# Operand addresses, a stage hand-over and a weight conversion with a part on GpSimd

## The chip, the cores and the metric

The kernel runs on one core of a Trainium2 chip. The metric is the device time of one execution in microseconds, as the median of several runs. The engines are called TensorE (PE), VectorE (DVE), ScalarE (ACT), GpSimd (POOL) and SyncE (SP, which issues all DMAs here).

## The reference

Three blocks follow each other; everything is float32, the weights come as float64.

```python
# attention: 8 batches, 8 heads, 576 tokens, head size 64; keys and values averaged over 8 tokens (72 remain)
attn = softmax(q @ mean8(k).T / 8)
x = attn @ mean8(v)                       # -> 4608 tokens x 512
# first block, d_ff = 768
h = maximum(maximum(x @ w1, x @ w2), x @ w3)
x = h @ w_out                             # 4608 x 512
# second block, d_ff = 2048
h = x @ w_in
out = (h - tanh(h)) @ w_out2              # 4608 x 512
```

## The kernel before

**Precision.** TensorE takes float32r operands. So every operand is kept as two tiles, H (the value rounded to float32r) and L (the rest), and each product is three matmuls, H with H, H with L and L with H, added up in one PSUM accumulator. A tile is split by a copy on ScalarE (H) and a subtraction on VectorE or GpSimd (L).

**Weight conversion** (`conv`, L74 to L90). A float64 weight tile arrives as pairs of 32-bit words (`raw`, 128x512 pairs, two buffers, loaded by `conv_load`). VectorE cuts the exponent out (L78), ScalarE turns it into a float32 exponent (L80), VectorE builds mantissa and sign (L81, L83, L85) and ORs the exponent in (L87); ScalarE rounds to H (L89), GpSimd subtracts to L (L90). `pe` and `ma` have two buffers each. One call does a whole tile; 18 tiles of w1, w2, w3, 6 of the first w_out and 32 of the second block go through it.

**Stages.**
- First stage (to about 628 us): the attention, tile by tile of up to 128 tokens, and the three products of the first block, in 12 blocks of 384 tokens. One product of 128 output columns is a "group" (`moe_group`, L466): 12 matmuls of 384 columns (L476 to L478), then a copy or a maximum (L480, L482). `moe_part` (L489) interleaves the groups with the attention's steps. Ahead of a group it calls `conv_next`, which converts one tile; `CONV_LEAD = 2` tiles are converted ahead of the first group. The first 18 groups are two blocks' first nine each, and need the nine first weight tiles alone. The six tiles of the first w_out are converted in the last block's groups.
- Middle stage (L540 to L604): 9 blocks of 512 tokens, `acc[e] += wo[kc] * h[kc]`, 72 matmuls of 512 columns a block (L592 to L594) in 6 steps kc. The h tiles come back from DRAM by `load_split` (L558), four steps ahead, and are split two steps ahead (ScalarE L566, VectorE L567). The sums go out by L598 and L600 and the DMA L601 into xs. Even blocks accumulate in the PSUM pool psm, odd ones in ps2. In the same loop `conv_c` converts the 32 tiles of the second block, evenly over the steps.
- Last stage (L612 on): 9 blocks of 512 tokens by 16 chunks of 128 hidden columns: `h2` (L657, 12 matmuls into one accumulator of pool psc), the activation `gact` (L631, 4 operations of ScalarE, 7 of VectorE and the cast L650), and `prod` three chunks later (L667, 4 sums of 3 matmuls). Its x tiles are loaded by `c_load` and split by `c_split`, the L part on GpSimd; those of the first block right at the start of the stage (L687 to L690), the others one block ahead.

**Order.** Each engine and each DMA queue runs its list in order. The lists are made by the framework, which takes an instruction as soon as its model of the program holds it ready, in the order of the source otherwise; so instructions of a later source line can stand ahead of others. Waits are put in from the tiles that are read and written.

**Addresses.** Tiles lie in stacks from both ends of a partition's memory. The first 16,384 bytes are a scratch area for DMA descriptors. Pools of the left side (consts, wH, wL, xH, xL, h, the conversion's buffers of the first stage, and the second block's weights ct) follow upwards: all operands of TensorE on this side start at 192 mod 512 bytes. Pools of the right side (the attention's `at`, then io, wo, the conversion's buffers of the middle stage, gp) go down from the end: io, wo and gp (ioH, ioL, woH, woL, gH, gL) all start at 480 mod 512. The attention's tiles are of other sizes, so their starts differ among themselves (VH, VL at 96, eH, eL, eX at 352).
In the groups both operands lie left, in the middle stage both right. In `h2` the stationary tile is ct (left) and the moving one io (right), in `prod` the stationary tile is gp's (right) and the moving one ct (left).

Of the kernel before, what the change touches and what calls it, by code (L numbers as in the profile page):

```python
# [36 lines left out]
CONV_LEAD = 2  # L37
# [10 lines left out]
def moe_chain_kernel(ctx, tc, qt, kt, vm, vl, ident, cst, w123, wo1, win, wout, out):  # L48
# [19 lines left out]
    # float64 words to float32, split into two float32r parts  # L68
    def conv_load(st, src):
        raw = st.tile([128, 512, 2], I32, tag="raw", name="raw", bufs=2)  # L70
        Q.dma_start(out=raw.bitcast(I64).rearrange("p n o -> p (n o)"), in_=src)
        return raw

    def conv(st, raw, H, L, eng):  # L74
        pe = st.tile([128, 512], I32, tag="pe", name="pe", bufs=2)
        a = st.tile([128, 512], I32, tag="ma", name="ma", bufs=2)
        lo, hi = raw[:, :, 0], raw[:, :, 1]
        V.tensor_scalar(out=pe, in0=hi, scalar1=20, scalar2=0x7FF,  # L78
                        op0=ALU.logical_shift_right, op1=ALU.bitwise_and)
        A.activation(pe, pe, AF.Relu, bias=ebias, scale=float(1 << 23))  # L80
        V.tensor_scalar(out=a, in0=hi, scalar1=3, scalar2=0x7FFFFF,  # L81
                        op0=ALU.logical_shift_left, op1=ALU.bitwise_and)
        V.scalar_tensor_tensor(out=a, in0=hi, scalar=-2147483648, in1=a,  # L83
                               op0=ALU.bitwise_and, op1=ALU.bitwise_or)
        V.scalar_tensor_tensor(out=a, in0=lo, scalar=29, in1=a,  # L85
                               op0=ALU.logical_shift_right, op1=ALU.bitwise_or)
        V.tensor_tensor(out=a, in0=a, in1=pe, op=ALU.bitwise_or)  # L87
        w = a.bitcast(F32)
        A.copy(H, w)  # L89
        eng.tensor_tensor(out=L, in0=w, in1=H.bitcast(F32), op=ALU.subtract)  # L90

# [5 lines left out]
    sta = pool("sta")  # L97
    at = pool("at", side="right")
# [18 lines left out]
    # attention units: (first token, tiles of tokens); a tile is (batch, first token in batch, count)  # L117
# [201 lines left out]
    # one list of steps for the whole attention, in the order in which they are issued  # L319
# [87 lines left out]
    # v of a batch may be replaced once its last product is issued  # L407
# [17 lines left out]
    # startup  # L425
# [10 lines left out]
    raws = {0: conv_load(sta, w123[0])}  # L436
    Q.dma_start(out=idt, in_=ident)
    raws[1] = conv_load(sta, w123[1])
# [4 lines left out]
    nconv = [0]  # L443

    def conv_next():
        i = nconv[0]
        if i < 18:
            conv(sta, raws.pop(i), wH[i].rearrange("p a b -> p (a b)"),
                 wL[i].rearrange("p a b -> p (a b)"), G)
            nconv[0] += 1  # L450
            if i + 2 < 18:
                raws[i + 2] = conv_load(sta, w123[i + 2])

# [9 lines left out]
    for _ in range(CONV_LEAD):  # L463
        conv_next()
# [24 lines left out]
    def moe_part(groups, upto):  # L489
        """groups of products, with the attention's steps up to upto spread over them"""  # L490
        first = pos[0]

        def pace(x):
            attn_to(first + (upto - first) * x // (2 * len(groups)))

        for k, (j, f, m) in enumerate(groups):
            conv_next()
            moe_group(j, f, m, lambda: pace(2 * k + 1))
            pace(2 * k + 2)
# [6 lines left out]
    def point(x):  # L506
        """the step at which the attention is x blocks far"""
# [7 lines left out]
    moe_part(gr(1, 0, HF), point(2.5))  # L515
# [9 lines left out]
    raws = {i: conv_load(sta, wo1[i]) for i in range(2)}  # L525
    nconv[0] = 0

    def conv_next():
        i = nconv[0]
        if i < NF:  # L530
            conv(sta, raws.pop(i), woH[i], woL[i], G)
            nconv[0] += 1
            if i + 2 < NF:
                raws[i + 2] = conv_load(sta, wo1[i + 2])

# [9 lines left out]
    # pairs in the order of use: input chunk c, output chunk c  # L545
    srcs = [(win if c % 2 == 0 else wout)[c // 2] for c in range(2 * NC2)]
    raws = {i: conv_load(stb, srcs[i]) for i in range(2)}
    nconv = [0]

    def conv_c():  # L550
        i = nconv[0]
        if i < 2 * NC2:
            conv(stb, raws.pop(i), wt[i][0], wt[i][1], G)
            nconv[0] += 1
            if i + 2 < 2 * NC2:
                raws[i + 2] = conv_load(stb, srcs[i + 2])
# [18 lines left out]

    loads = [(j, kc) for j in range(NB) for kc in range(NF)]
# [6 lines left out]
    for i, (j, kc) in enumerate(loads):  # L583
        if kc == 0:
            acc = [psm.tile([128, 512], F32, tag="mm", name="ps_mm") if j % 2 == 0 else
                   ps2.tile([128, 512], F32, tag="sc" if e < 2 else "tr", name="ps_acc") for e in range(NE)]
# [17 lines left out]
        while nconv[0] < min(2 * NC2, (i + 1) * 2 * NC2 // (len(loads) - 2)):  # L604
            conv_c()
# [7 lines left out]
    gp = pool("gp", bufs=2, side="right")  # L613
    xl_ = [(j, kc) for j in range(NB) for kc in range(NE)]
    lt = {}
    nld, nsp = [0], [0]

    def c_load():
# [145 lines left out]
```

## Time and profile before

| | |
|---|---|
| median of 3 runs | 1607.62 us (1607.29 to 1608.44) |
| span of the profiled execution | 1608.5 us |
| another time of that execution | none is shown |
| TensorE busy | 1548.1 us (96%) |
| VectorE busy | 1215.2 us (76%) |
| ScalarE busy | 836.4 us (52%) |
| GpSimd busy | 223.7 us (14%) |

The span is cut into 40 slices of 40.2 us; a digit is the busy share of a slice in tenths (9 is 90% or more), and PEclk the clock granted to TensorE in tenths of full speed.

```profile
PE   4789999999999999998899999999999999999999
DVE  8999565555555663999588878788888888887886
POOL 5351210202010011332301001010101001010000
PEclk9899999999999999999999999999999999999999
```

A matmul's profiled duration overlaps the next one's, so what a matmul costs is read from the distance of starts, or from the number of matmuls in a stretch without idle time. Likewise an instruction of VectorE that is held up by another engine shows as a longer one.

### The profile page before, as it was taken

What the parts mean: (1) busy time and instruction counts of PE and PEld (TensorE: products, weight loads), DVE (VectorE), ACT (ScalarE), POOL (GpSimd) and SP (SyncE); (2) the same over time, 40 slices, a digit from 0 to 9 for tenths busy, and PEclk for the clock granted to TensorE, in tenths of its full rate; (3) what the DMA queues carried; (4) which work ended last, traced back from release to release, by engine and by line L of the source; (5) the groups of instructions that cost most, each with busy time, mean ns of one, the idle gap of its engine ahead of it and who ended that gap; (6) DMA issues with size and microseconds to landing.
All of it is one profiled execution on the core that took longest, in us unless ns stands there. A gap on an engine that the chain in (4) does not pass through costs nothing.

```text
span 1608.5 us, 21497 instructions
## 1 busy us (share of the span) xinstructions
PE 1548.1 (96%) x7540; PEld 1337.7 (83%) x7540; DVE 1215.2 (76%) x2131; ACT 836.4 (52%) x2081; POOL 223.7 (14%) x245
## 2 busy tenths in 40 slices
PE   4789999999999999998899999999999999999999
PEld 4688999999999999876688888888888888888887
DVE  8999565555555663999588878788888888887886
ACT  5565455545545521444465555555555555555554
POOL 5351210202010011332301001010101001010000
PEclk9899999999999999999999999999999999999999
DMA  7455232212121232676500001010100000010000
GB/s 236 158 161 163 84 99 79 87 45 75 42 65 39 67 120 77 230 241 234 198 1 27 26 2 52 1 53 0 33 21 27 26 27 27 1 54 0 27 1 27
DMA packets 61997, 117.87 MB, mean 73 GB/s; under 512 B 10816, under 2 KB 20160, under 8 KB 61888
## 3 DMA queue, kind: packets, MB, share of 16 engines
q1 hardware_dynamic: 61888, 116.49, 21.8%
q8 instruction: 59, 0.97, 0.3%
q14 instruction: 50, 0.41, 0.1%
HBM read 83.43 MB, written 33.03 MB: 72 GB/s over the span
## 4 chain that ended last, share of the span: by engine, by line
PE 50%; DVE 0%; issue 0%
PE ps_mm L663 8%; PE ps_mm L662 8%; PE ps_mm L664 8%; PE ps_acc L676 8%; PE ps_acc L675 8%; PE ps_acc L677 8%; DVE ob L683 0%
## 5 line engine op out<-in xcount | busy, mean ns | idle before, releaser
L476 PE MATMUL ps_mm<-xH,wH 128*128 128x384 f32 x864 | 304.5, 353 | 5.3 <-ACT wH L89 4.5
L477 PE MATMUL ps_mm<-xL,wH 128*128 128x384 f32 x864 | 292.4, 339 | 1.0 <-DVE xL L317 1.0
L478 PE MATMUL ps_mm<-xH,wL 128*128 128x384 f32 x864 | 292.7, 339 | 0.6 <-POOL wL L90 0.6
L650 ACT CAST gH<-w 128x512 fp32r<-128x512 f32 x144 | 89.4, 621 | 297.0 <-DVE w L649 297.0
L662 PE MATMUL ps_mm<-ioH,ctH 128*128 128x512 f32 x576 | 228.3, 396 | 5.3 <-ACT ob L598 5.3
L663 PE MATMUL ps_mm<-ioL,ctH 128*128 128x512 f32 x576 | 229.1, 398 | 0.0
L664 PE MATMUL ps_mm<-ioH,ctL 128*128 128x512 f32 x576 | 228.5, 397 | 0.0
L675 PE MATMUL ps_acc<-ctH,gH 128*128 128x512 f32 x576 | 228.1, 396 | 0.0
L676 PE MATMUL ps_acc<-ctL,gH 128*128 128x512 f32 x576 | 227.9, 396 | 0.0
L677 PE MATMUL ps_acc<-ctH,gL 128*128 128x512 f32 x576 | 227.9, 396 | 0.0
L651 DVE TENSOR_TENSOR gL<-w,gH 128x512 fp32r<-128x512 f32 x144 | 104.1, 723 | 92.5 <-ACT gH L650 92.3
L476 PEld LDWEIGHTS ps_mm<-xH,wH 128*128 128x128 f32 x864 | 164.7, 191 | 7.2 <-ACT wH L89 4.8
L477 PEld LDWEIGHTS ps_mm<-xL,wH 128*128 128x128 f32 x864 | 164.6, 191 | 1.9 <-DVE xL L317 1.7
L478 PEld LDWEIGHTS ps_mm<-xH,wL 128*128 128x128 f32 x864 | 163.7, 189 | 1.5 <-POOL wL L90 1.5
L567 POOL TENSOR_TENSOR ioL<-ioL,ioH 128x512 fp32r<-128x512 f32 x36 | 53.5, 1509 | 666.9 <-ACT ioH L566 666.9
L662 PEld LDWEIGHTS ps_mm<-ioH,ctH 128*128 128x128 f32 x576 | 108.6, 189 | 32.2 <-ACT ob L598 5.7
L663 PEld LDWEIGHTS ps_mm<-ioL,ctH 128*128 128x128 f32 x576 | 108.7, 189 | 27.1
L664 PEld LDWEIGHTS ps_mm<-ioH,ctL 128*128 128x128 f32 x576 | 108.8, 189 | 26.0
L675 PEld LDWEIGHTS ps_acc<-ctH,gH 128*128 128x128 f32 x576 | 108.2, 188 | 26.5
L677 PEld LDWEIGHTS ps_acc<-ctH,gL 128*128 128x128 f32 x576 | 108.2, 188 | 26.5
L676 PEld LDWEIGHTS ps_acc<-ctL,gH 128*128 128x128 f32 x576 | 108.2, 188 | 25.8
L482 DVE TENSOR_TENSOR h<-h,ps_mm 128x384 f32<-128x384 f32 x144 | 79.0, 549 | 66.0 <-PE ps_mm L478 59.2
(108 smaller groups left out, 2924.9 us busy)
## 6 DMA issues: line engine op xcount, KB each, us to landing
hs<-h SPq DMA_DIRECT2D x72, 192.0 KB, 1.9
ioL<-hs SPq DMA_DIRECT2D x54, 256.0 KB, 4.2
kraw<-kt SPq DMA_DIRECT2D x32, 288.0 KB, 3.9
raw<-w SPq DMA_DIRECT2D x18, 512.0 KB, 3.5
xs<-ob SPq DMA_DIRECT2D x36, 256.0 KB, 2.6
ioL<-xs SPq DMA_DIRECT2D x36, 256.0 KB, 3.0
out<-ob SPq DMA_DIRECT2D x36, 256.0 KB, 2.2
qraw<-qt SPq DMA_DIRECT2D x32, 256.0 KB, 2.7
```

The source lines that it names most:

```text
L476: T.matmul(ps[:, :BA], wH[i][:, kc], xh[:, kc], start=(kc == 0), stop=False)
L477: T.matmul(ps[:, :BA], wH[i][:, kc], xl[:, kc], start=False, stop=False)
L478: T.matmul(ps[:, :BA], wL[i][:, kc], xh[:, kc], start=False, stop=(kc == NE - 1))
L482: V.tensor_tensor(out=t, in0=t, in1=ps[:, :BA], op=ALU.max)
L650: A.copy(gH, w)
L651: V.tensor_tensor(out=gL, in0=w, in1=gH.bitcast(F32), op=ALU.subtract)
L662: T.matmul(ps, wh[:, kc], xh, start=(kc == 0), stop=False)
L663: T.matmul(ps, wh[:, kc], xl2, start=False, stop=False)
L664: T.matmul(ps, wl_[:, kc], xh, start=False, stop=(kc == NE - 1))
L675: T.matmul(acc, gH[:, r], oh, start=(c == 0), stop=False)
L676: T.matmul(acc, gH[:, r], ol, start=False, stop=False)
L677: T.matmul(acc, gL[:, r], oh, start=False, stop=(c == NC2 - 1))
```

## The change

- **Addresses.** A tile of 72 floats (288 bytes a partition), used by nothing, is put at the bottom of the right side, so that all tiles there start 288 bytes lower: io, wo and gp at 192 mod 512, as the left side does. The scratch area for DMA descriptors becomes 1,024 bytes instead of 16,384 (both multiples of 512).
- **Conversion in three steps** (class `Conv`). `bits` is L78 to L85 with the exponent on ScalarE, `join` adds the exponent on GpSimd (an int32 add in the place of VectorE's OR, L87), `split` is the copy to H on ScalarE and the subtraction on GpSimd. A call of `step` splits tile i-2, takes the bits of tile i, loads tile i+2 and joins tile i-1. `pe` has three buffers and `ma` four.
- **Pace.** `CONV_LEAD` is 4 steps. In the second nine groups a step is made ahead of every second group.
- **First tiles of the last stage.** In the last four steps of the middle stage `c_load(V)` loads the four x tiles of block 0, and in the last two `c_split` splits them, the L part on VectorE; the calls ahead of the last stage are gone.
- **PSUM.** In the middle stage even blocks accumulate in ps2 and odd ones in psm; the last block is an even one.

```diff
-CONV_LEAD = 2
+CONV_LEAD = 4
...
+    class Conv:
+        def __init__(self, st, srcs, outs):
+            self.st, self.srcs, self.outs, self.n = st, srcs, outs, len(srcs)
+            self.raws, self.w, self.i = {}, {}, 0
+            for i in range(2):
+                self.load(i)
...
+        def bits(self, i):
+            raw = self.raws.pop(i)
+            pe = self.st.tile([128, 512], I32, tag="pe", name="pe", bufs=3)
+            a = self.st.tile([128, 512], I32, tag="ma", name="ma", bufs=4)
...
+        def join(self, i):
+            a, pe = self.w[i]
+            G.tensor_tensor(out=a, in0=a, in1=pe, op=ALU.add)
+
+        def split(self, i):
+            w = self.w.pop(i)[0].bitcast(F32)
+            H, L = self.outs[i]
+            A.copy(H, w)
+            G.tensor_tensor(out=L, in0=w, in1=H.bitcast(F32), op=ALU.subtract)
+
+        def step(self):
+            i = self.i
+            if i >= self.n + 2:
+                return
+            if i - 2 >= 0:
+                self.split(i - 2)
+            if i < self.n:
+                self.bits(i)
+                self.load(i + 2)
+            if 0 <= i - 1 < self.n:
+                self.join(i - 1)
+            self.i += 1
...
+    pool("rp", side="right").tile([128, 72], F32, name="rpad")
     at = pool("at", side="right")
...
         for k, (j, f, m) in enumerate(groups):
-            conv_next()
+            if k % every == 0:
+                cv.step()
...
-    moe_part(gr(1, 0, HF), point(2.5))
+    moe_part(gr(1, 0, HF), point(2.5), 2)
...
-            acc = [psm.tile([128, 512], F32, tag="mm", name="ps_mm") if j % 2 == 0 else
+            acc = [psm.tile([128, 512], F32, tag="mm", name="ps_mm") if j % 2 else
...
         if i + AHEAD < len(loads):
             lt[i + AHEAD] = load_split(hsrc(*loads[i + AHEAD]), V)
-        while nconv[0] < min(2 * NC2, (i + 1) * 2 * NC2 // (len(loads) - 2)):
-            conv_c()
+        else:
+            c_load(V)
+        if i >= len(loads) - 2:
+            c_split()
+            c_split()
+        while cv.i < min(cv.n + 2, (i + 1) * (cv.n + 2) // (len(loads) - 2)):
+            cv.step()
...
-    for _ in range(4):
-        c_load()
-    for _ in range(4):
-        c_split()
...
-    nc = bacc.Bacc("TRN2", target_bir_lowering=False, num_devices=1)
+    nc = bacc.Bacc("TRN2", target_bir_lowering=False, num_devices=1, dynamic_dma_scratch_size=1024)
```

## Rows read from the trace of the kernel before

**Rows 1.** The page's first lines: span, busy us, share, instructions by engine.

```profile
span 1608.5 us, 21497 instructions
...
PE 1548.1 (96%) x7540; PEld 1337.7 (83%) x7540; DVE 1215.2 (76%) x2131; ACT 836.4 (52%) x2081; POOL 223.7 (14%) x245
```

**Rows 2.** Three stretches: busy us (x instructions) by engine, TensorE's granted clock, DMA.

```profile
40.00:160.00 120.00, 100.69 (x551) 93.02 (x551) 116.73 (x234) 72.56 (x250) 44.00 (x49) 0.90 0.50 160
...
560.00:600.00 40.00, 39.14 (x224) 38.55 (x224) 26.85 (x47) 12.20 (x22) 8.05 (x4) 1.00 0.40 136
628.10:789.50 161.40, 152.31 (x648) 120.17 (x648) 148.13 (x213) 72.55 (x124) 48.94 (x33) 1.00 0.65 223
```

**Rows 3.** Waits of TensorE, 628 to 790 us: total us, times, longest.

```profile
PE ps_mm L593 <- DVE ioL L567: 4.1, 6, 1.5
PE ps_acc L593 <- DVE ioL L567: 4.0, 7, 1.5
```

**Rows 4.** The same columns in three stretches where TensorE never waits.

```profile
600.00:626.00 26.00, 26.00 (x152) 26.00 (x151) 4.43 (x8) 1.93 (x4) 0.00 (x0) 1.00 0.09 31
632.00:700.00 68.00, 68.00 (x302) 56.31 (x301) 65.19 (x93) 30.81 (x53) 22.74 (x15) 1.00 0.67 228
820.00:1590.00 770.00, 770.00 (x3301) 619.30 (x3300) 632.51 (x982) 423.39 (x735) 44.81 (x29) 1.00 0.06 21
```

**Rows 5.** Groups of TensorE instructions: busy us, mean ns of one, idle us before.

```profile
L675 PE MATMUL ps_acc<-ctH,gH 128*128 128x512 f32 x576 | 228.1, 396 | 0.0
...
L594 PE MATMUL ps_mm<-ioH,woL 128*128 128x512 f32 x120 | 46.8, 390 | 0.0
```

**Rows 6.** Timeline around the last stage's start: start us, us, engine, line.

```profile
787.02 2.73 SPq L561 DMA_DIRECT2D ioL<-xs  x6
...
789.54 0.39 PE L594 MATMUL ps_mm<-ioH,woL 128*128 128x512 f32 x1
...
790.88 3.30 ACT L566 CAST ioH<-ioL 128x512 fp32r<-128x512 f32 x5 [6.17 <-DMA ioL<-xs]
...
795.21 0.79 PE L662 MATMUL ps_mm<-ioH,ctH 128*128 128x512 f32 x1 [5.27 <-ACT ob L598]
```

**Rows 7.** Busy times and granted clock (PEclk) behind that start.

```profile
795.30:801.20 5.90, 5.90 (x14) 4.64 (x15) 0.00 (x0) 0.71 (x2) 3.70 (x3) 0.50 0.67 222
```

**Rows 8.** Groups of VectorE and GpSimd instructions, 628 to 790 us.

```profile
L90 POOL TENSOR_TENSOR ctL<-ma,ctH 128x512 fp32r<-128x512 f32 x32 | 47.6, 1490 | 157.8 <-ACT ctH L89 157.8
...
L567 DVE TENSOR_TENSOR ioL<-ioL,ioH 128x512 fp32r<-128x512 f32 x47 | 44.2, 943 | 6.8 <-ACT ioH L566 6.8
...
L85 DVE SCALAR_TENSOR_TENSOR ma<-raw,ma 128x512 int32<-128x512 int32 x30 | 26.5, 883 | 0.6
...
L81 DVE TENSOR_SCALAR ma<-raw 128x512 int32<-128x512 int32 x30 | 22.4, 746 | 1.2 <-POOL ctL L90 1.2
...
L87 DVE TENSOR_TENSOR ma<-ma,pe 128x512 int32<-128x512 int32 x30 | 20.5, 682 | 0.5
```

**Rows 9.** Single lines: duration ns min/median/max, first and last start.

```profile
L81 DVE TENSOR_SCALAR ma<-raw x56: 409/418/1520, 14.4 to 778.5; 128x512 int32<-128x512 int32 x56
...
L85 DVE SCALAR_TENSOR_TENSOR ma<-raw,ma x56: 672/691/1776, 16.4 to 779.6; 128x512 int32<-128x512 int32 x56
...
L567 DVE TENSOR_TENSOR ioL<-ioL,ioH x54: 674/684/1795, 562.0 to 784.0; 128x512 fp32r<-128x512 f32 x54
...
L90 POOL TENSOR_TENSOR ctL<-ma,ctH x32: 1282/1358/1826, 632.3 to 782.3; 128x512 fp32r<-128x512 f32 x32
```

**Rows 10.** Timelines of VectorE and GpSimd at 652 us.

```profile
652.27 1.51 DVE L81 TENSOR_SCALAR ma<-raw 128x512 int32<-128x512 int32 x1
...
652.14 1.35 POOL L90 TENSOR_TENSOR ctL<-ma,ctH 128x512 fp32r<-128x512 f32 x1 [3.68 <-ACT ctH L89]
```

**Rows 11.** Timeline of TensorE at 335 us: an av product.

```profile
335.31 0.34 PE L309 MATMUL ps_av<-eH,VH 128*128 128x384 f32 x1
...
336.01 0.34 PE L476 MATMUL ps_mm<-xH,wH 128*128 128x384 f32 x1
```

More of the change, by code (lines that the diff above doesn't have):

```diff
@@ L66, in moe_chain_kernel @@
     xs = [dr.tile([NE, 128, BB], F32, name=f"xs{i}") for i in range(NB)]
[L69 to L90, printed above, removed]
@@ L435, in moe_chain_kernel @@
     next_v()
-    raws = {0: conv_load(sta, w123[0])}
+    cv = Conv(sta, [w123[i] for i in range(18)],
+              [tuple(t[i].rearrange("p a b -> p (a b)") for t in (wH, wL)) for i in range(18)])
     Q.dma_start(out=idt, in_=ident)
-    raws[1] = conv_load(sta, w123[1])
     q_split(0)
@@ L487, in moe_chain_kernel, with moe_part @@
     hsb = {}
-    def moe_part(groups, upto):
+    def moe_part(groups, upto, every=1):
         first = pos[0]
@@ L524, in moe_chain_kernel @@
     woL = [wo.tile([128, 512], F32R, name=f"woL{i}") for i in range(NF)]
[L525 to L534, printed above, removed]
+    cv = Conv(sta, [wo1[i] for i in range(NF)], list(zip(woH, woL)))
     moe_part(gr(NA - 1), pos[0])
@@ L546, in moe_chain_kernel @@
     srcs = [(win if c % 2 == 0 else wout)[c // 2] for c in range(2 * NC2)]
[L547 to L556, printed above, removed]
+    cv = Conv(stb, srcs, wt)
     def load_split(src, eng):
@@ L574, in hsrc, with c_load, c_split @@
         return hs[g][kc][:, o:o + BB]
+    xl_ = [(j, kc) for j in range(NB) for kc in range(NE)]
+    ct = {}
+    nld, nsp = [0], [0]
+    def c_load(eng):
+        i = nld[0]
+        if i < len(xl_):
+            j, kc = xl_[i]
+            ct[i] = load_split(xs[j][kc], eng)
+            nld[0] += 1
+    def c_split():
+        i = nsp[0]
+        if i < len(xl_):
+            ct[i][1]()
+            nsp[0] += 1
     loads = [(j, kc) for j in range(NB) for kc in range(NF)]
@@ L603, in moe_chain_kernel @@
             lt[i + AHEAD] = load_split(hsrc(*loads[i + AHEAD]), V)
-        while nconv[0] < min(2 * NC2, (i + 1) * 2 * NC2 // (len(loads) - 2)):
-            conv_c()
+        else:
[4 more added lines that the diff above has]
+        while cv.i < min(cv.n + 2, (i + 1) * (cv.n + 2) // (len(loads) - 2)):
+            cv.step()
     close("stb")
@@ L613, in moe_chain_kernel @@
     gp = pool("gp", bufs=2, side="right")
[L614 to L618, printed above, removed]
-        i = nld[0]
-        if i < len(xl_):
-            j, kc = xl_[i]
-            lt[i] = load_split(xs[j][kc], G)
-            nld[0] += 1
-    def c_split():
-        i = nsp[0]
-        if i < len(xl_):
-            lt[i][1]()
-            nsp[0] += 1
     def gact(ps):
@@ L660, in h2 @@
         for kc in range(NE):
[L661 removed]
+            xh, xl2 = ct[j * NE + kc][0]
             T.matmul(ps, wh[:, kc], xh, start=(kc == 0), stop=False)
@@ L701, in moe_chain_kernel @@
                 for _ in range(NE):
-                    c_load()
+                    c_load(G)
             if 6 <= c < 10:
@@ L706, in moe_chain_kernel @@
                 for k in range(NE):
-                    lt.pop(j * NE + k)
-    for nme in ("psc", "gp", "io", "wl", "cst"):
+                    ct.pop(j * NE + k)
+    for nme in ("psc", "gp", "io", "rp", "wl", "cst"):
         close(nme)
```

27 lines of the change are left out of this document (16 added, 11 removed).

## The prediction

> **What bounds the kernel now.** I read the summary first: TensorE is busy 1548.1 of 1608.5 us [rows 1], so whatever is won must come from matmuls that run faster or from places where they wait. A change of about 0.2% (3 us) is what a measurement here can tell from none. The 40 slices, which stand with the times, show TensorE short of full at the start and around the middle stage (the second product). The busy times of those stretches say who is full there: VectorE, 116.7 of 120 us from 40 to 160 us; and in the middle stage, 628.1 to 789.5 us, 148.1 of 161.4 us, where TensorE's 648 matmuls need less [rows 2]. What TensorE waits for there is VectorE's split L567, 8.1 us in 13 waits [rows 3]. So the start and the middle stage go at VectorE's pace. The last stage (from 795 us) is TensorE alone: 3301 matmuls of 512 columns are counted in 770 us, the first already running, without a gap: one each 233.3 ns [rows 4].
>
> The middle stage has matmuls of the same form, and in its first stretch, where nothing waits, 302 are counted in 68 us, two of them already running: one each 226.7 ns [rows 4]. In clocks of 2.4 GHz that is 544 against 560 for the same 512 columns. One difference between the two stages is where operands lie: in the middle stage stationary and moving tiles are both on the right side (480 mod 512), in the last stage one of them lies left (192) and the other right (480).
>
> **The change, part by part.**
>
> *Addresses.* The pad of 288 bytes moves every right-side tile from 480 to 192 mod 512, so in the last stage the two operands agree as they do in the middle stage. The last stage has 6 groups of 576 matmuls, 3456 in all [rows 5]. Nothing in the trace of before shows that stage with equal addresses: its slot is bounded by 233.3 ns (nothing gained) and 226.7 ns (the middle stage's). I take 226.7, since the nearest row has the same columns, the same weight loads and the same triplets of products: 3456 x 6.67 ns = **-23.0 us**. VectorE is no new bound: it is busy 632.5 of 770 us there [rows 4], and a stage 3% shorter leaves it near 85%. In the first two stages the operands of a matmul all move together or not at all, so nothing changes there. The smaller descriptor area only gives room; no DMA here comes from GpSimd.
>
> What the 6.67 ns are is not seen in the trace, and the Trainium skill speaks against it: "TensorE: Matmul & The Clock Gate", step-by-step section of part 2, has two independent read ports, so that loading the next weights takes no read bandwidth from the running matmul. By that rule the sum loses its 23.0 us; the two rates of rows 4 differ all the same.
>
> *Hand-over to the last stage.* Before, TensorE stands 5.27 us in front of the first L662 matmul, put down to ScalarE's output copies L598; ahead of those in its queue are five casts L566 that waited 6.17 us for the loads from xs, issued at 787.02, 2.5 us ahead of the last L594 [rows 6]. Then the granted clock is 0.50, the lower level, from 795.3 to 801.2 us: 14 matmuls in 5.9 us instead of 3.3 at 233 ns, so 2.6 us more [rows 7]. After the change these four loads and their splits are issued in the last four steps of the middle stage, and the last block's sums lie in the other PSUM pool, so that the first accumulator of the last stage has long been free. On SP's queue the loads pass the last block's stores, which nobody awaits, and still stand behind those of the block before. Two of the four splits follow VectorE's last output copies: I leave 2 x 0.6 = 1.2 us of waiting for them and take -5.3 - 2.6 + 1.2 = **-6.7 us** (bounds: 0 if the wait stays, -7.9).
>
> *Joining on GpSimd, middle stage.* VectorE loses L87, 32 times 0.68 us: -21.8 us [rows 8]. GpSimd gets 32 more instructions of the kind of L90 (1.36 us median, 1.49 mean) [rows 8, 9]. They are not free for VectorE: while a GpSimd product runs, VectorE's next instruction is held. At 652.14 us L90 starts, and L81, which has a median of 0.42 us, takes 1.51 us [rows 9, 10]. Summed over the stage, mean against undisturbed median of the three lines most hit: L81 30 x (746 - 418), L85 30 x (883 - 691), L567 47 x (943 - 684) ns, together 27.8 us for 32 GpSimd products [rows 8, 9]: 0.87 us each. TensorE needs 648 x 226.7 ns = 146.9 of the stage's 161.4 us and VectorE paces the rest, so what VectorE gains or loses I put on the stage in full. A join's price has never been seen; bounds are 0 (it falls where VectorE reads PSUM or is idle) and 1.49 (held for a whole mean L90). I take 0.87, the mean of a like instruction in the same stage: 32 x (0.87 - 0.68) = +6.1 us. Two more tiles can be through VectorE's four steps before the stage begins (four "ma" buffers instead of two, and VectorE has a third of 560 to 600 us free [rows 2]): 2 x 2.2 = -4.4; four splits of the last stage's tiles now run here: 4 x 0.68 = +2.7. Sum **+4.4 us**. The wait that joins add is GpSimd's on ScalarE's L80; a step later ScalarE's cast waits for the join, with casts L566 behind it in its queue. One whole step of run-up, about 5 us (161.4 / 32), hides both.
>
> The Trainium skill, "SBUF — State Buffer", section on who interferes with whom, says that of a VectorE instruction with two SBUF inputs and a GpSimd one that reads SBUF the second is blocked fully. By that a join would cost up to its whole 1.36 us and this stage +20 us instead of +4.4; rows 10 show 1.09 us, since the instruction in flight goes on.
>
> *Joining on GpSimd, start.* 18 tiles at the same price: 18 x (0.87 - 0.68) = **+3.4 us** (bounds 18 x -0.68 = -12.2 and 18 x 0.81 = +14.6). Four lead steps give as many finished tiles ahead of each group as two whole conversions did, and spreading the second nine groups' steps moves no VectorE work past 160 us: nothing. The six tiles of woH fall where VectorE has room (26.9 of 40 us) [rows 2]: nothing; were that room gone, 6 x 0.19.
>
> *Sum.* -23.0 - 6.7 + 4.4 + 3.4 = -21.9 us on the profiled execution. Its span is 1608.5, 0.9 us above the median of the runs (1607.62) and 0.1 above the slowest; no other end-to-end time is shown for it. On the median: **1585.7 us**.
>
> **The rivals.**
> 1. *Addresses do nothing.* The slot of 233.3 ns comes from something else of the last stage. For: the av products of the first stage have operands at 96 and 352 mod 512, and four of 384 columns take 0.70 us, 175 ns each [rows 11], hardly more than the 173.3 ns of a group product with equal addresses (150 starts in 26 us) [rows 4]. Against: the second product of the last stage has triplets into one sum like the middle stage's, and yet a mean duration of 396 ns, not 390 [rows 5]. Time: 1607.6 - 6.7 + 7.8 = 1608.7. The port rule above gives the same.
> 2. *Joins hide.* VectorE is freed and the middle stage becomes TensorE's: 146.9 instead of 161.4 us, -14.5; the start gains up to 12.2, say 6. 1607.6 - 29.7 - 14.5 - 6 = 1557.4. Against: the 0.87 us that an L90 costs VectorE now.
> 3. *Joins hold VectorE to the end* (slower). Join and split stand back to back on GpSimd, and VectorE is held through both. At 1.49 us: middle 32 x 0.81 - 1.7 = +24.2, start +14.6: 1607.6 - 29.7 + 38.8 = 1616.7. It decides from a price of 1.31 us on, where 50 x (1.31 - 0.68) - 1.7 uses up the 29.7. Against: the hold of 1.09 us [rows 10].
> 4. *The hand-over keeps its wait*, because the last splits come behind VectorE's backlog: 1607.6 - 23.0 + 7.8 = 1592.4.
>
> **How the numbers follow.** Forecast 0.52, rival 1 0.15, rival 2 0.13, rival 3 0.12, rival 4 0.08. Faster by over 0.2% (under 1604.4): the forecast, rivals 2 and 4, and 0.04 of rivals 1 and 3, whose other terms may come out lower: 0.77. Within 0.2%: 0.07 of rival 1 and 0.03 of rival 3, 0.10. Slower: their remaining 0.13. The range reaches up to 1612 (past rival 1, short of rival 3) and down to 1565 (joins at 0.46 us: 50 x 0.41 = 20.5 less, the upper half of rival 2); outside it lie most of rival 3 and half of rival 2, with a little of rival 1, 0.2. The forecast's own range is 1576 to 1602 (joins at 0.68 to 1.2 us).
>
> **What would show it.** In the last stage starts 226.7 ns apart (3397 in 770 us): addresses right; 233.3: rival 1; anything between: the rule is finer than mod 512. Little idle time in front of the first L662 and no lower clock behind it: hand-over right. In the middle stage, from the first L592 to the last L594: 160 to 171 us says the join's price is near 0.9; near 148 rival 2; over 180 rival 3, with VectorE's mean times of L81, L85 and L567 grown. In the start, VectorE full for a little longer than to 160 us. I am wrong if the last stage keeps its slot, or if the middle stage moves by more than 15 us either way.

## The result and the profile after

The changed kernel takes **1625.47 us** (median of 4 runs, 1623.99 to 1626.78), the kernel before 1607.90 (4 runs, 1607.29 to 1608.44): 1.0106 times as long, 95% interval 1.0092 to 1.0121. The forecast was 1585.7; the outcome lies past the range, on the slow side. The profiled execution is the fastest of the four, 1623.99 us with a span of 1622.2.

The span falls into four pieces at three starts of TensorE: the first product of the middle stage, its last one, and the first of the last stage. Forecast is the sum's term for each.

| piece (us) | before | after | difference | forecast |
|---|---|---|---|---|
| first stage | 628.1 | 644.8 | +16.7 | +3.4 |
| middle stage, first to last start | 161.4 | 188.7 | +27.3 | +4.4 |
| from there to the last stage | 5.7 | 1.2 | -4.5 | -5.3 + 1.2 |
| last stage to the end of the span | 813.3 | 787.5 | -25.8 | -23.0 - 2.6 |
| sum | 1608.5 | 1622.2 | +13.7 | -21.9 |

Two terms came as forecast, two did not. The page's busy line and slices after (against [rows 1] and the slices shown with the times):

```profile
span 1622.2 us, 21552 instructions
...
PE 1538.2 (95%) x7540; PEld 1348.7 (83%) x7540; DVE 1216.8 (75%) x2079; ACT 832.8 (51%) x2081; POOL 292.8 (18%) x297
...
PE   4679999999999999987799999999999999999999
...
DVE  7999554656555581889758888888888888888886
...
POOL 5763202102010030655400101010000101010000
PEclk9779999999999999998899999999999999999999
```

The two places where TensorE was short of full before are wider now, and TensorE's clock is lowered in both. The same stretches as in [rows 2], the middle stage at its new place, and 700 us of the last stage:

```profile
40.00:160.00 120.00, 93.31 (x475) 85.15 (x474) 114.87 (x205) 66.45 (x232) 70.94 (x70) 0.82 0.54 170
560.00:600.00 40.00, 37.15 (x202) 35.63 (x201) 33.75 (x47) 14.86 (x30) 16.16 (x12) 0.96 0.43 140
644.80:833.90 189.10, 162.80 (x649) 127.63 (x648) 148.05 (x179) 74.77 (x130) 90.68 (x62) 0.94 0.58 193
850.00:1550.00 700.00, 700.00 (x3090) 579.63 (x3089) 589.77 (x923) 395.38 (x691) 45.40 (x29) 1.00 0.07 23
```

In the middle stage VectorE is busy 148.05 us, to a tenth what it was before, though it runs 34 instructions fewer; but the stage is 27.3 us longer, so VectorE now stands idle for 41 us where it stood some 14. In the last stage 3090 matmuls start in 700 us, 226.5 ns each.

What each engine waits for in that stage (after, 644.8 to 834 us: total us, times, longest):

```profile
ACT ctH L106 <- POOL ma L101: 71.2, 28, 6.3
POOL ctL L107 <- ACT ctH L106: 69.7, 29, 49.2
POOL ma L101 <- DVE ma L95: 42.0, 25, 3.4
DVE ioL L570 <- ACT ioH L569: 31.3, 13, 4.2
...
PE ps_mm L612 <- ACT ioH L569: 10.8, 3, 5.2
```

Read from the bottom it is one chain: TensorE waits for ScalarE's cast of an h tile, VectorE's split L570 for the same cast, ScalarE stands ahead of it at the cast of a weight tile, which waits for the join on GpSimd, which waits for VectorE. The timelines of ScalarE, GpSimd, VectorE and TensorE around one such turn show it instruction by instruction:

```profile
793.87 0.72 ACT L90 ACTIVATE pe<-pe,consts 128x512 int32<-128x512 int32 x1 [2.38 <-DVE pe L88]
794.96 0.62 ACT L106 CAST ctH<-ma 128x512 fp32r<-128x512 f32 x1 [0.37 <-POOL ma L101]
798.98 0.62 ACT L106 CAST ctH<-ma 128x512 fp32r<-128x512 f32 x1 [3.40 <-POOL ma L101]
799.50 2.69 ACT L569 CAST ioH<-ioL 128x512 fp32r<-128x512 f32 x5
...
797.68 1.26 POOL L101 TENSOR_TENSOR ma<-ma,pe 128x512 int32<-128x512 int32 x1 [0.62 <-DVE ma L95]
...
795.97 1.64 DVE L95 SCALAR_TENSOR_TENSOR ma<-raw,ma 128x512 int32<-128x512 int32 x1
800.15 1.96 DVE L570 TENSOR_TENSOR ioL<-ioL,ioH 128x512 fp32r<-128x512 f32 x2 [2.54 <-ACT ioH L569]
...
794.53 0.39 PE L614 MATMUL ps_mm<-ioH,woL 128*128 128x512 f32 x1
800.17 0.79 PE L612 MATMUL ps_mm<-ioH,woH 128*128 128x512 f32 x1 [5.25 <-ACT ioH L569]
```

ScalarE reaches the second L106 at 795.6 and stands 3.40 us, until the join that began at 797.68 is done; five casts of h tiles, whose loads landed between 794.5 and 798.7, wait behind it, and TensorE waits 5.25 us. Its next matmul takes 0.79 us instead of 0.39: from 800.2 to 806.0 us the granted clock is 0.50, the lower level. In the source, join and cast are one step apart. In ScalarE's queue they are not: of the 31 casts to H that have a next tile, 22 stand there ahead of that tile's exponent step L90, as many as in the kernel before with its one step.

The hand-over after, TensorE's timeline (against [rows 6]):

```profile
833.47 0.39 PE L614 MATMUL ps_acc<-ioH,woL 128*128 128x512 f32 x1
834.69 0.47 PE L670 MATMUL ps_mm<-ioH,ctH 128*128 128x512 f32 x1 [0.83 <-ACT ioH L569]
```

### The profile page after: what moved, and what is told of

Its sections match the earlier page's. It is cut to its first block, busy times and chain, and to the rows that moved or that the text cites. A ratio compares the mean times of both kernels' runs of the same rounds, so it can differ in the third digit from the quotient of the medians.

```text
span 1622.2 us, 21552 instructions
## 1 busy us (share of the span) xinstructions
PE 1538.2 (95%) x7540; PEld 1348.7 (83%) x7540; DVE 1216.8 (75%) x2079; ACT 832.8 (51%) x2081; POOL 292.8 (18%) x297
## 4 chain that ended last, share of the span: by engine, by line
PE 81%; DVE 11%; POOL 3%; issue 2%; DMA 2%; ACT 1%; SPq 0%; DVEq 0%; ACTq 0%; POOLq 0%
PE ps_mm L497 9%; PE ps_mm L499 8%; PE ps_mm L498 8%; PE ps_mm L670 8%; PE ps_acc L685 8%; PE ps_mm L672 8%; PE ps_acc L683 8%; PE ps_mm L671 8%; PE ps_acc L684 8%; DVE ma L93 2%; DVE pe L88 1%; DVE ma L95 1%; POOL ma L101 1%; DVE ioL L570 1%; DVE ma L91 1%
## 5 line engine op out<-in xcount | busy, mean ns | idle before, releaser
L497 PE MATMUL ps_mm<-xH,wH 128*128 128x384 f32 x864 | 306.1, 355 | 6.1 <-ACT wH L106 2.8
L670 PE MATMUL ps_mm<-ioH,ctH 128*128 128x512 f32 x576 | 224.2, 389 | 0.8 <-ACT ioH L569 0.8
L672 PE MATMUL ps_mm<-ioH,ctL 128*128 128x512 f32 x576 | 224.1, 389 | 0.0
L683 PE MATMUL ps_acc<-ctH,gH 128*128 128x512 f32 x576 | 224.1, 389 | 0.0
L684 PE MATMUL ps_acc<-ctL,gH 128*128 128x512 f32 x576 | 224.1, 389 | 0.0
L671 PE MATMUL ps_mm<-ioL,ctH 128*128 128x512 f32 x576 | 224.1, 389 | 0.0
L685 PE MATMUL ps_acc<-ctH,gL 128*128 128x512 f32 x576 | 224.1, 389 | 0.0
L497 PEld LDWEIGHTS ps_mm<-xH,wH 128*128 128x128 f32 x864 | 165.5, 192 | 8.2 <-DVE h L503 3.3
L570 POOL TENSOR_TENSOR ioL<-ioL,ioH 128x512 fp32r<-128x512 f32 x32 | 49.3, 1556 | 670.5 <-ACT ioH L569 670.5
L670 PEld LDWEIGHTS ps_mm<-ioH,ctH 128*128 128x128 f32 x576 | 108.0, 188 | 23.5 <-ACT ioH L569 1.2
L684 PEld LDWEIGHTS ps_acc<-ctL,gH 128*128 128x128 f32 x576 | 108.1, 188 | 22.4
```

What stands on the lines that cost most here:

```text
L497: T.matmul(ps[:, :BA], wH[i][:, kc], xh[:, kc], start=(kc == 0), stop=False)
L670: T.matmul(ps, wh[:, kc], xh, start=(kc == 0), stop=False)
L671: T.matmul(ps, wh[:, kc], xl2, start=False, stop=False)
L672: T.matmul(ps, wl_[:, kc], xh, start=False, stop=(kc == NE - 1))
L683: T.matmul(acc, gH[:, r], oh, start=(c == 0), stop=False)
L684: T.matmul(acc, gH[:, r], ol, start=False, stop=False)
```

## The experiments

**First set: undo one part, do one part.** The join back on VectorE (`e1`), the addresses alone (`e2`), the hand-over alone (`e3`), and the ring cut in ScalarE's queue (`e6`).

```diff
 # e1: in the changed kernel
-            G.tensor_tensor(out=a, in0=a, in1=pe, op=ALU.add)
+            V.tensor_tensor(out=a, in0=a, in1=pe, op=ALU.bitwise_or)
 # e6: in the changed kernel; ScalarE's instructions in the block stay behind "last"
+            self.last = A.activation(pe, pe, AF.Relu, ...)   # in bits
-            if i - 2 >= 0:
-                self.split(i - 2)
             if i < self.n:
                 self.bits(i)
                 self.load(i + 2)
+            if i - 2 >= 0:
+                with tc.issue_after(self.last.ins):
+                    self.split(i - 2)
```

> The changed kernel with the join alone put back on VectorE (the OR of before, in the step i-1); addresses, hand-over, three steps and pace stay. Chain theory (the join on GpSimd puts VectorE, GpSimd and ScalarE into one ring of waits, because ScalarE's queue holds the cast to H right behind the join, and the casts for the moving tiles behind that): the middle stage falls from 189.1 us to 158 to 165, the first stage ends at 626 to 634 us instead of 644.8, the time is 1574 to 1584. Rival, price theory (each GpSimd instruction simply holds VectorE for most of its time): the same here. Rival, order theory (the 16.7 us of the first stage come from four lead steps and from the spreading over every second group, not from the join): the middle stage falls, the first stage still ends at 640 or later, the time is 1588 to 1595.

> The kernel before with the addresses alone (pad of 288 bytes, smaller descriptor area). If operands at equal addresses are what the last stage gained: slot 226.7 instead of 233.3 ns, 3456 x 6.67 = 23 us, time 1583 to 1587, first two stages unchanged. If something else of the changed kernel did it: 1606 to 1609.

> The kernel before with the hand-over alone (first four x tiles loaded and split in the middle stage, PSUM pools swapped). From the distance last product of the middle stage to the first of the last (5.66 to 1.22 us) and the low clock behind it (2.6 us): -7, plus up to 2.7 for four more splits on VectorE in the middle stage: time 1599 to 1604, slot of the last stage 233.3 ns. If the distance shrank only because the slower middle stage gave the loads time: -3 or less, 1604 to 1608.

> The changed kernel with the order within a step made binding: the cast to H (and the rest of the split) of tile i-2 stays behind the exponent step of tile i in ScalarE's queue, so that the join of that tile has one whole step to finish. All instructions and the join on GpSimd stay. Chain theory: ScalarE no longer waits for the join (71 us, 28 times, in the changed kernel), the middle stage falls from 189.1 to 160 to 172 us, the first stage ends at 628 to 636, time 1580 to 1600. Price theory: GpSimd's work is unchanged, so the middle stage stays at 185 to 190 us and the time at 1620 to 1627.

Measured, against 1608.92 us before (13 runs):

| | time | ratio (95%) | first stage to | middle stage | to the last stage |
|---|---|---|---|---|---|
| e1 join on VectorE | 1581.30 | 0.9834 (0.9819 to 0.9848) | 631.1 | 161.3 | 1.22 |
| e2 addresses alone | 1585.41 | 0.9859 (0.9843 to 0.9876) | 625.8 | 162.5 | 5.37 |
| e3 hand-over alone | 1609.65 | 1.0007 (0.9998 to 1.0016) | 628.5 | 162.9 | 5.62 |
| e6 casts kept behind | 1622.08 | 1.0088 (1.0073 to 1.0103) | 649.5 | 183.4 | 1.22 |

(Here and below the middle stage is counted to the end of its last product: 161.8 us before, 189.1 after.) e1 settles that the join costs the changed kernel 44 us in all, 27.8 in the middle stage and 13.7 in the first; of the first stage's 16.7 us about 3 belong to lead, pace or steps, as far as one trace each can tell (e2, e3, e9 and the other pads, which have the first stage of before, end it between 625.5 and 628.5 us). e2 gives the addresses their full 23 us by themselves. e3 gives nothing at all, which neither expectation had. And e6 is a miss: ScalarE's wait for the join falls from 71.2 us to 3.9, and the middle stage gets only 5.7 us shorter. VectorE is then busy 154.1 us and idle 29.

**Second set: the price of GpSimd's products, and the hand-over.** `e7` is e1 with one int32 add on GpSimd for each tile that nobody reads; `e8` is e1 with the subtraction to L on VectorE too; `e9` is e3 with the conversion ending three steps earlier; `e5` is the kernel before with the join on GpSimd in its one-step conversion.

```diff
 # e7: in split, with the join on VectorE
+            G.tensor_tensor(out=d, in0=w.bitcast(I32), in1=w.bitcast(I32), op=ALU.add)
 # e8: in split, with the join on VectorE
-            G.tensor_tensor(out=L, in0=w, in1=H.bitcast(F32), op=ALU.subtract)
+            V.tensor_tensor(out=L, in0=w, in1=H.bitcast(F32), op=ALU.subtract)
 # e9: on top of e3
-        while nconv[0] < min(2 * NC2, (i + 1) * 2 * NC2 // (len(loads) - 2)):
+        while nconv[0] < min(2 * NC2, (i + 1) * (2 * NC2 + 2) // (len(loads) - 2)):
 # e5: in the kernel before
-        V.tensor_tensor(out=a, in0=a, in1=pe, op=ALU.bitwise_or)
+        G.tensor_tensor(out=a, in0=a, in1=pe, op=ALU.add)
```

> The kernel with the join on VectorE, and on GpSimd, in every split, one int32 add of the same size whose result nobody reads. It has the GpSimd load of the changed kernel (two products for each tile) without any engine waiting for the join. Price theory (a GpSimd product takes about 1.06 us out of VectorE's time where VectorE is full; an OR took 0.60): VectorE, busy 140.8 of 161.3 us in the middle stage, gets up to 32 x 1.06 = 34 us more, of which its idle 20 us can take a part: middle stage 177 to 193 us, first stage ending 8 to 20 us later than 631.1, time 1605 to 1635. Ring theory (the waits for the join are the cost, the load itself little): middle stage under 172 us, time under 1595.

> The kernel with the join on VectorE, and the subtraction to L of the conversion on VectorE as well, so that GpSimd does none of the conversion. Price theory: each of these products costs VectorE 0.60 us in place of 1.06, 32 x 0.46 = 15 us in the middle stage, which then comes to TensorE's own 147 to 153 us; the first stage ends 3 to 8 us earlier than 631.1; time 1560 to 1572. Ring theory (a GpSimd product costs VectorE little): 32 x 0.60 = 19 us more on a VectorE that is nearly full: middle stage 172 to 180 us, time 1590 to 1605.

> The kernel before with the hand-over (which alone gave nothing, 5.62 us between the stages) and one number changed: the conversion in the middle stage runs to the pace of 34 tiles in 52 steps instead of 32, so that its last tile comes three steps earlier, as the three-step class does it. Theory that the hand-over needs VectorE and ScalarE free of the conversion in the last steps: distance between the stages 1 to 2.5 us, no low clock behind it, time 1598 to 1604. Rival, that something else of the changed kernel shortened it: distance 5 to 6 us, time 1607 to 1612.

> The kernel before with the join alone moved to GpSimd, in the old conversion of one step. If the three steps give the join no run-up (in the order that the framework made for the changed kernel, 24 of the 32 casts to H of the middle stage stand ahead of the next tile's exponent step, as without steps): middle stage 183 to 195 us like the changed kernel's 189.1, first stage ending at 638 to 650, time 1640 to 1660. If the steps do shorten the ring: middle stage 198 us or more, time over 1660. If neither ring nor steps matter and only the price of 1.06 against 0.60 us counts: middle stage 173 to 180 us, time 1625 to 1638.

(The last text counts 24 casts; the trace of the changed kernel has 22 of 31.) Measured, against 1608.76 us (18 runs):

| | time | ratio (95%) | first stage to | middle stage | to the last stage |
|---|---|---|---|---|---|
| e7 idle add | 1610.67 | 1.0012 (1.0002 to 1.0021) | 642.1 | 178.1 | 1.22 |
| e8 split on VectorE | 1567.54 | 0.9746 (0.9721 to 0.9771) | 628.9 | 147.1 | 3.29 |
| e9 hand-over, early end | 1608.27 | 0.9997 (0.9988 to 1.0007) | 627.0 | 165.0 | 3.81 |
| e5 join on GpSimd, one step | 1646.27 | 1.0235 (1.0220 to 1.0250) | 646.8 | 186.2 | 1.22 |

The middle stage of e1, e7 and e8, one row each:

```profile
631.10:792.40 161.30, 152.01 (x650) 120.51 (x648) 140.75 (x207) 75.36 (x129) 52.43 (x34) 1.00 0.66 225
```

```profile
642.10:820.20 178.10, 159.59 (x649) 123.31 (x648) 160.53 (x207) 75.23 (x129) 90.39 (x62) 0.97 0.60 204
```

```profile
628.90:776.00 147.10, 147.10 (x650) 121.48 (x648) 130.87 (x237) 73.13 (x125) 0.00 (x0) 1.00 0.74 245
```

From e1 to e7 VectorE runs the same 207 instructions and is busy 19.8 us longer, for 28 more products on GpSimd: **0.71 us each**. From e1 to e8 it runs 30 more instructions and is busy 9.9 us less. Groups of VectorE in the middle stage, e1 and then e8, show where:

```profile
L570 DVE TENSOR_TENSOR ioL<-ioL,ioH 128x512 fp32r<-128x512 f32 x51 | 43.0, 853 | 14.9 <-ACT ioH L569 14.6
L95 DVE SCALAR_TENSOR_TENSOR ma<-raw,ma 128x512 int32<-128x512 int32 x28 | 25.8, 921 | 0.3
...
L88 DVE TENSOR_SCALAR pe<-raw 128x512 int32<-128x512 int32 x26 | 16.9, 649 | 2.0 <-DMA raw<-wout 1.6
```

```profile
L570 DVE TENSOR_TENSOR ioL<-ioL,ioH 128x512 fp32r<-128x512 f32 x50 | 34.2, 686 | 13.6 <-ACT ioH L569 13.5
L107 DVE TENSOR_TENSOR ctL<-ma,ctH 128x512 fp32r<-128x512 f32 x32 | 21.7, 684 | 0.7 <-ACT ctH L106 0.7
L95 DVE SCALAR_TENSOR_TENSOR ma<-raw,ma 128x512 int32<-128x512 int32 x28 | 19.2, 684 | 0.2
L101 DVE TENSOR_TENSOR ma<-ma,pe 128x512 int32<-128x512 int32 x28 | 19.1, 683 | 0.0
...
L88 DVE TENSOR_SCALAR pe<-raw 128x512 int32<-128x512 int32 x26 | 10.9, 420 | 1.4 <-DMA raw<-wout 0.6 <-DMA raw<-win 0.6
```

Without GpSimd no VectorE instruction is held any more, and TensorE runs the stage without a gap at 227 ns a matmul. But 0.71 us is little more than an OR's own place in VectorE's queue (L101 shows 0.68 us, and the next instruction starts 0.60 us after it), so a price of this size can't make the changed kernel's stage 27 us longer: rival 3's time came, its mechanism did not. An estimate over all of GpSimd's products goes from e8's 130.87 us, less 0.60 us for each instruction that the other kernel runs fewer: 27.9 us are left for e1's 34 products and 52.0 for the changed kernel's 62, 0.82 and 0.84 us each. e5 says that the three steps gave the join nothing: the stage is about as long without them (186.2), and the time is the changed kernel's plus the missing 23 us of the addresses, within 3 us. It also has the distance of 1.22 us to the last stage, though nothing of the hand-over is changed in it.

**Third set: the order in VectorE's queue, and a better version.** e6 left VectorE idle at the end of the stage, and so does the changed kernel. VectorE's timeline of the changed kernel behind its last conversion instruction, the L95 at 795.97 shown above:

```profile
800.15 3.77 DVE L570 TENSOR_TENSOR ioL<-ioL,ioH 128x512 fp32r<-128x512 f32 x5 [2.54 <-ACT ioH L569]
803.84 1.28 DVE L620 COPY ob<-ps_acc 128x512 f32<-128x512 f32 x2
805.03 0.68 DVE L570 TENSOR_TENSOR ioL<-ioL,ioH 128x512 fp32r<-128x512 f32 x1
809.91 2.01 DVE L570 TENSOR_TENSOR ioL<-ioL,ioH 128x512 fp32r<-128x512 f32 x3 [4.20 <-ACT ioH L569]
```

VectorE's conversion ends at 797.6, 36 us ahead of the stage's end, with 15 splits L570 still behind it, four of them of x tiles; behind the last such instruction there were 3 in the kernel before, which has no x tiles there, and 10 in e1. TensorE has then run 516 of its 648 matmuls (571 in e1). So VectorE converts tiles that nobody needs yet while TensorE waits for h tiles. `e12` slows the pace in the source; `e14` and `e15` also bind the conversion behind the h split of the same step in VectorE's queue, with the ring cut (e14) and left (e15). `e10` and `e11` have nothing of the conversion on GpSimd and issue the last stage's x loads eight steps earlier: e10 on the three-step class, e11 on the conversion of before. `e13`, `e16` and `e17` are e2 with other pads.

```diff
 # e12: on top of e6; two more calls of step behind the loop
-        while cv.i < min(cv.n + 2, (i + 1) * (cv.n + 2) // (len(loads) - 2)):
+        while cv.i < min(cv.n + 2, (i + 1) * (cv.n + 2) // (len(loads) + 2)):
 # e15: the pace of e12 in the changed kernel, and (e14: on top of e6)
+            vs[0] = eng.tensor_tensor(out=l, ...)   # in load_split
+            with tc.issue_after(vs[0].ins):
                 cv.step()
 # e10, e11: the x loads of the last stage, with ioL in 10 buffers
-        else:
+        if NF * (NB - 2) <= i < NF * (NB - 2) + NE:
             c_load(V)
 # e13, e16, e17: 136, 56 and 40 floats
-    pool("rp", side="right").tile([128, 72], F32, name="rpad")
+    pool("rp", side="right").tile([128, 136], F32, name="rpad")
```

> The changed kernel with the casts kept behind (which took ScalarE's wait for the join away and yet left 183.4 us), and the conversion spread over all 54 steps of the middle stage instead of 52 less two. Order theory (once the ring is cut, VectorE is full for 148 us and then idle 21 of the last 35, since its queue holds the conversion four steps ahead of the products): the idle end shrinks, middle stage 168 to 178 us, time 1606 to 1617. Rival, that VectorE's time for GpSimd's products alone sets the stage: 181 to 185 us and 1619 to 1625 as before.

> The changed kernel with the casts kept behind, the slower pace, and VectorE's queue bound as well: each step's conversion stays behind the split of the h tile of the same step, so the conversion can't run ahead of the products' needs. Order theory: VectorE's 154 us of work and some 10 of idle time make the middle stage, 162 to 172 us, and the idle end is under 10 us; time 1598 to 1612. Price theory (GpSimd's products alone set it): 181 to 186 us, 1618 to 1626.

> The changed kernel with VectorE's queue bound to the source order in the same way and the slower pace, while ScalarE's casts H stay where the framework puts them, so that the ring stays. If order alone makes the stage long: 162 to 172 us, like the run beside it. If the ring costs by itself: 175 to 190 us, ScalarE's wait for the join 60 us or more. Time 1596 to 1610 or 1612 to 1627.

> The kernel with join and split of the conversion on VectorE, and the four x loads of the last stage issued in the first four steps of block 7, thus ahead of that block's stores in SyncE's queue instead of behind them (with two more buffers for them). Theory that the hand-over hung on the loads' place in that queue: distance between the stages 0.3 to 1.5 us instead of 3.29, no low clock behind it, middle stage still 147 us, time 1560 to 1566. Rival, that it hangs on ScalarE's and VectorE's last output copies: distance 3 us as before, time 1565 to 1570.

> The kernel before with addresses, hand-over with early loads as in the run beside it, and the subtraction to L of the conversion on VectorE; the conversion of one step, its lead of two tiles and its pace are those of before. Theory that three steps and the lead of four bring nothing once GpSimd is out (VectorE full is VectorE full): middle stage 147 to 149 us, first stage ending at 620 to 627 us (625.8 with the addresses alone, less what GpSimd's 18 products held), time 1555 to 1563. Rival, that the three steps are what keeps the middle stage at TensorE's pace: middle stage 152 us or more, time over 1565.

> The kernel before with the addresses alone, but a pad of 544 instead of 288 bytes: right side at 448, left side at 192, so that the last stage's operands differ by 256 mod 512. If only equality mod 512 counts: slot of the last stage 233.3 ns, as with the difference of 288, time 1606 to 1610. If equality mod 256 or less is enough: 226.7 ns and 1583 to 1587. Between: the cost depends on the distance.

> The kernel before with the addresses alone, and a pad of 224 bytes: right side at 256, left at 192 mod 512, a difference of 64 (288 costs, 0 and 256 do not). If equality mod 64 is enough: slot of the last stage 226.7 ns, time 1583 to 1587. If it has to be mod 256 or 128: 233.3 ns and 1606 to 1610.

> The same with a pad of 160 bytes: right side at 320, a difference of 128 mod 512. If equality mod 128 or less is enough: 226.7 ns, 1583 to 1587. If it has to be mod 256: 233.3 ns, 1606 to 1610.

Measured, against 1608.97 us (e10 to e13) and 1607.77 us (e14 to e17). The other pads were run once each: e13 took 1586.75 us, e16 1603.95 and e17 1607.20.

| | time | ratio (95%) | first stage to | middle stage | to the last stage |
|---|---|---|---|---|---|
| e12 ring cut, slow pace | 1622.67 | 1.0088 (1.0074 to 1.0102) | 647.0 | 185.4 | 1.22 |
| e15 order bound | 1619.98 | 1.0076 (1.0059 to 1.0092) | 643.9 | 172.6 | 11.87 |
| e14 order bound, ring cut | 1613.29 | 1.0035 (1.0018 to 1.0053) | 645.0 | 164.4 | 12.50 |
| e10 three steps, no GpSimd | 1563.95 | 0.9724 (0.9711 to 0.9738) | 626.4 | 147.1 | 1.22 |
| e11 one step, no GpSimd | 1561.41 | 0.9706 (0.9693 to 0.9719) | 625.2 | 147.1 | 1.22 |

e12 says nothing on the order: 15 splits stand behind the last conversion instruction as in e6, so the edit never reached VectorE's queue. e14 and e15 reach it (2 splits behind), and cut the two causes one by one. The middle stage of e15 and of e14:

```profile
643.90:816.50 172.60, 157.31 (x649) 124.45 (x647) 134.58 (x177) 70.67 (x122) 83.02 (x58) 0.96 0.62 203
```

```profile
645.00:809.40 164.40, 154.25 (x650) 123.01 (x648) 136.06 (x176) 70.31 (x121) 85.11 (x56) 0.98 0.65 213
```

The ring is left whole in e15, and ScalarE's wait for the join with it (71.2 us in the changed kernel):

```profile
ACT ctH L106 <- POOL ma L101: 71.1, 27, 3.8
```

VectorE's idle end is gone. The last 35 us of the stage in the changed kernel, e15 and e14 (the third busy time of a row is VectorE's):

```profile
798.80:833.80 35.00, 33.04 (x132) 26.46 (x132) 13.77 (x20) 13.85 (x24) 4.00 (x4) 0.90 0.49 156
```

```profile
781.50:816.50 35.00, 30.33 (x119) 22.86 (x117) 28.09 (x38) 14.35 (x25) 17.52 (x13) 0.95 0.64 205
```

```profile
774.40:809.40 35.00, 32.13 (x134) 24.82 (x132) 31.43 (x40) 15.77 (x28) 19.27 (x13) 0.98 0.65 208
```

From 189.1 us the order alone takes 16.5 (e15), the ring alone 5.7 (e6), both 24.7 (e14). But these figures are upper bounds for what the order cost, since part of the work has only moved. Both bound kernels end some conversion instructions behind the stage, issue the fourth of the x loads only when the last product has started (the changed kernel 10.7 us ahead of that), and let the x tiles' casts stand behind the last weight tiles', so that the hand-over takes 12 us. Counted from the stage's first product to the first of the last stage, the way is 167.1 us before, 189.9 after, 162.1 in e1, 184.2 in e6, 184.1 in e15 and 176.5 in e14: the order alone takes 5.8, the ring alone 5.7, both 13.4 of the 27.8 us that the join costs there. So each of the two is a cause, which is the larger isn't shown, and between 3 us (164.4 against e1's 161.3) and 14.4 us is left to neither. Neither kernel is faster than before. Nor did either come out as expected: e15's 172.6 us lies between its two ranges, and e14's 1613.29 us just past its 1598 to 1612.

The last stage, 850 to 1550 us, with a difference between the operands of 288 bytes (before; 32 mod 256), 0 (e2), 256 (e13), 64 (e16) and 128 (e17), in this order:

```profile
850.00:1550.00 700.00, 700.00 (x3002) 563.00 (x3001) 575.91 (x892) 385.85 (x671) 44.81 (x29) 1.00 0.07 23
```

```profile
850.00:1550.00 700.00, 700.00 (x3090) 579.82 (x3089) 587.40 (x919) 394.13 (x689) 45.33 (x29) 1.00 0.07 23
```

```profile
850.00:1550.00 700.00, 700.00 (x3090) 579.83 (x3089) 586.73 (x917) 394.40 (x689) 45.37 (x29) 1.00 0.07 23
```

```profile
850.00:1550.00 700.00, 700.00 (x3023) 568.43 (x3023) 578.45 (x899) 387.53 (x675) 44.77 (x29) 1.00 0.07 23
```

```profile
850.00:1550.00 700.00, 700.00 (x3005) 563.62 (x3004) 576.65 (x893) 385.88 (x670) 44.79 (x29) 1.00 0.07 23
```

That is 233.2, 226.5, 226.5, 231.6 and 232.9 ns a matmul. A difference of 256 is as good as none; 64, 128 and 288 cost.

## Why the prediction was wrong

*Addresses: right, and shown.* 226.5 ns where 226.7 was taken from the middle stage [rows 4], 25.8 us less in the last stage with the low clock's 2.6 in it; e2 gives 1585.41, which is 23.5 below its before. Rival 1 is out. The Trainium skill's rule of two independent read ports ("TensorE: Matmul & The Clock Gate", step-by-step section of part 2), by which loading weights takes no read bandwidth from the running matmul, gives no reason for the five rows above to differ. They do, from 226.5 to 233.2 ns, and the measurement decides.

*Hand-over: right in size, wrong in cause.* The distance fell to 1.22 us as forecast, but not because four loads were moved: alone they bring nothing (e3). In SyncE's queue they stand right behind the stores of block 7, whose copies come late. From the issue of the fourth load to the last stage's first product pass 7 to 8 us: issued 1.6 us ahead of the last product's start (e3, as before) the distance is 5.62, at 3.5 (e9) 3.81, at 4.9 (e8) 3.29, at 6.4 (e1) and 7.0 (e5) 1.22. With the loads ahead of those stores (e10) it is 1.22 too, where e8 had 3.29. The changed kernel passed that point because its middle stage is slow at the end; e5 passed it so too, with the hand-over of before. Nor do the swapped PSUM pools show in e3, where TensorE's wait (5.2 us) is still put down to ScalarE's output copies. The sum named block 7's stores on that queue and then dropped them; that was the step that failed, though its number came out.

*Joining, price: right.* A join was priced 0.87 us of VectorE's time; an added product of the same size measured 0.71 (e7 against e1), and the estimate over all products is 0.8. The bound of 1.49, on which rival 3 stood, is far off. The OR that was taken off VectorE was priced too high, at its profiled 0.68 us: it holds up the next instruction by 0.60. "SBUF — State Buffer" in the Trainium skill has, of a VectorE instruction with two SBUF inputs and a GpSimd one that reads SBUF, the second fully blocked (section on who interferes with whom); the rows agree that instructions are held, on average for about half of the 1.33 us that an added product takes in e7's middle stage.

*Joining, middle stage: wrong.* +27.3 us instead of +4.4, past the 15 us that the prediction itself had named as its sign of being wrong. Two sentences failed. "One whole step of run-up, about 5 us (161.4 / 32), hides both": there was no run-up, because the framework, not the source, orders the queues, and put the cast of a tile ahead of the next tile's exponent step in 22 of 31 cases; ScalarE stood 71.2 us at the join. And "what VectorE gains or loses I put on the stage in full": VectorE's busy time did not move (148.1 us [rows 2] and 148.05), but it stopped being what paces the stage. With the OR gone, the framework put the conversion earlier into VectorE's queue, ahead of the splits that TensorE waits for. e6, e14 and e15 show that the ring and this order each cost time: within the stage the ring takes 6 to 8 us and the order 16.5 to 19, with the hand-over counted in each of them 6 to 8, and both together 13.4 of 27.8. How the rest divides stays open. That the framework chose this order because its model has GpSimd's products cost VectorE nothing is argued from the order alone, not shown.

What the order took from VectorE is less plain than its idle end suggests. Over the whole stage it stands idle 38.0 us in e15 and 28.3 in e14, little less than in the changed kernel (41.0) and e6 (29.2). What fell is its busy time, with 2079 instructions in each whole execution: from 1216.8 to 1203.9 us (e15) and from 1228.5 (e6) to 1210.2 (e14). So it was also held less by GpSimd; why isn't shown.

*Joining, start: wrong, and partly open.* +16.7 instead of +3.4. GpSimd's products alone make 11.0 (e7 against e1), where the sum had 18 x 0.87 less 18 x 0.68; taking the ORs off VectorE should have given most of that back, and did not. The changed kernel ends the stage another 2.7 later than e7, which is within the scatter of e6, e12 and e14 (649.5, 647.0 and 645.0 with the same source there). VectorE is still full from 40 to 160 us (114.87 of 120 us, with 29 instructions fewer than in [rows 2]). ScalarE's wait for the join is there too (22.4 us from 40 to 170 us), but cutting the ring did not help (e6: 649.5). The six tiles of the first w_out, for which the sum had nothing, were not free either: the 601st of the 864 matmuls of L497 starts 13.2 us later than before (480.6 against 467.4 us), and 3.5 us more are lost behind it, where they are converted. Whether the order is at fault in this stage as well was not tried.

*Rivals.* Rival 3 came nearest in time (1616.7) and in one mark (middle stage over 180 us), for a reason that it did not have; of its other mark, VectorE's means, L85 grew (883 to 1104 ns at L95) and L567 fell (943 to 892 at L570). Rival 4's outcome is what the hand-over alone gave (e3), though the wait hung on the loads and not on VectorE's last splits.

## What to carry to other kernels

Moving an instruction to another engine moves the waits of everything behind its consumer: read the consumer's queue in its real order, not in the source's, and ask what stands behind it (here ScalarE waited 71.2 us, with the casts of h tiles behind it). Where a framework orders queues, a freed engine may be filled with work that nobody needs yet; bind the order where it matters, check in the trace that the binding took, and count the next stage's start in, since a bound queue can move the cost there. The best version here goes the other way: nothing of the conversion on GpSimd, equal addresses, early x loads, in the conversion of before (e11, 1561.41 us, 0.9706 of the time before).

## What was not expected of the hardware

GpSimd's elementwise products were a loss for VectorE even where they were there from the start: without them VectorE did 30 more instructions in 9.9 us less busy time (e8 against e1), and the middle stage became TensorE's. And the operands of a matmul need not agree mod 512: 256 bytes apart cost nothing (226.5 ns), 64 cost 5.0 ns, 128 and 288 6.4 and 6.6 ns of each 512-column slot.
